# A fused state-space and long-convolution kernel: the first load in halves, table preparation shared out anew, K's spectrum ahead of V's

## The chip, the cores and the metric

One core of one Trainium2 chip. The metric is the device time of one execution in microseconds; the median of three runs of the kernel before is 444.19 (442.5 to 445.19). Times inside the kernel are counted from the start of the profiled span.

## The reference

Two branches read the same x and are mixed by a gate (2048 rows, 1024 channels, everything in bf16 outside, one batch):

```python
g = sigmoid((x * gate_w).sum(-1, keepdims=True))
# A: complex diagonal state space, P = 1024 states
Lam_bar = exp(dt * Lam);  B_bar = ((Lam_bar - 1) / Lam)[:, None] * Bmat
h_t = Lam_bar * h_(t-1) + x_t @ B_bar.T
a = 2 * real(h @ Cmat.T) + x * Dskip
# B: gated long convolution
k_shift = 4-tap causal filter of k (weights shift_k);  kv = k_shift * v
y = irfft(rfft(kv, 2S) * rfft(ssm_k, 2S))[:S] + kv * ssm_D
b = x * y
out = g * a + (1 - g) * b
```

## The kernel before

The convolution of branch B goes first, in eight chunks of 128 channels (`NC = 8`). It is a transform over 512-row blocks made of matrix products with tables of cosines and sines: `CF`, `SF` (forward; `NCF`, `NSF` are negated parts) and `CI`, `SI` (inverse, in two halves `h2`). For a chunk c the steps are:

- `load` fetches `kT`, `vT` (k and v transposed) and `kn` (the kernel ssm_k) by transposing DMAs on SyncE's queue.
- `taps` (lines 430 to 437): sixteen matmuls of `kT` with `dg`, four diagonal 128 x 128 matrices that hold the filter weights of the chunk, and two ScalarE evictions into `ks`. `dgs` (252 to 259) makes `dg`, four instructions, on VectorE for chunks 0 and 1 and on ScalarE for the others. Chunk 0 uses `first_times_v`, which multiplies by v straight from PSUM.
- `times_v`: two VectorE products, `lo` and `ks`.
- `fold_K`, `fold_V`: even and odd parts. `fold_V` multiplies by `PM`, four plus or minus identities; ScalarE evicts into `eok` and `eov`.
- `fwd_K(c, hf)`, `fwd_V(c, hf)`: the spectra, in two halves of frequencies. PSUM tiles `psk`, `psv`; ScalarE evicts them, two each, into `Kh` and `Vh`.
- `products(c, hf)` (511 to 544): the block products on VectorE, temporaries `t` from the rings `w4` (three buffers) and `u4` (four buffers), result `G`. It is a generator: its first step makes the products of lag 0, the rest comes later.
- `inverse(c)`: `psz`, sixteen matmuls a step with `CI` and `SI`, evicted to `cv` and written to DRAM.

After the eight chunks comes branch A: `Bu` (x times B), a rotated scan on VectorE over 16 pieces, `Cy` (states times C), the gate and the mixing. Its parameters are made by `state_params` (312 to 371), a generator on [128, 8] tiles: step 1 copies the columns into `pcol`, step 2 makes `dtv` and `rv` (ScalarE Exp) and `av`, `bv`, `thn` (VectorE), step 3 makes angles on VectorE (`thU`, `th_rq`, `th_fr`, `thU_rq`, `thU_fr`) and their sines and cosines on ScalarE (`th_fa` to `thU_cos`), and the rest makes the coefficients on VectorE (`rc` to `mc2i`). Exp and Sin lie in different ACT tables, and a table load stands wherever one follows the other. `turn_table` makes the rotation tables of branch A between the chunks.

The order of the work is written out by hand: `put` (line 97) ties every instruction to the one issued before it on the same engine, so the order of the calls is the order on each engine, and `step` and `run` drive the generators. A buffer of a ring is given to a new tile when its last reader is done; the reader's engine is then waited for. All PSUM work of a chunk shares three slots (`ps2`).

Before the loop stands the prologue: the first loads, nine matmuls on zeros (`raise_clock`), `dg` of chunk 0, the forward tables from `rqf` (fractions of turns; `hf` becomes |rqf| on VectorE and CF is its cosine), the first chunk up to its spectra, and `inverse_angles`, which makes the angles of the inverse tables in the rings `u4` and `w4`; the angles are read much later, by `inverse_table` in chunk 0 of the loop:

```python
def sincos(rq, n, sin_out, cos_out, sin_scale):
    fa = u4([128, n], F32, "fa")
    act(fa, rq, func=ACT.Abs)
    act(sin_out, rq, func=ACT.Sin, scale=sin_scale)
    act(cos_out, fa, func=ACT.Sin, bias=pih, scale=-TWO_PI)
```

Of the kernel before, what the change touches and what calls it, by code (L numbers as in the profile page):

```python
# [9 lines left out]
ALU = mybir.AluOpType  # L10
ACT = mybir.ActivationFunctionType
BF16 = mybir.dt.bfloat16
F32 = mybir.dt.float32
# [7 lines left out]
def kernel(  # L21
# [26 lines left out]
    nc = tc.nc  # L48
    xf = A_x.flatten_outer_dims()
    kf = B_k.flatten_outer_dims()  # L50
    vf = B_v.flatten_outer_dims()
    of = out.flatten_outer_dims()
    S, D = xf.shape
# [3 lines left out]
    ND = D // 128  # L57
    NP = P // 128
    NT = S // 128
    TB = 512  # L60
    NTB = S // TB
    NG = NP // 2
    NC = D // 128
# [5 lines left out]
    consts = pool("consts", 1)  # L69
# [4 lines left out]
    xt_pool = pool("xt", 2)  # L74
# [5 lines left out]
    def w4(shape, dt, name):  # L80
        return wk.tile(shape, dt, name=name, tag="w4")

    def u4(shape, dt, name):
        return wu.tile(shape, dt, name=name, tag="u4")
# [10 lines left out]
    def put(eng, f, *a, **kw):  # L95
        with tc.issue_after(prev[eng]) if eng in prev else nullcontext():
            i = f(*a, **kw)  # L97
        prev[eng] = getattr(i, "ins", i)
# [7 lines left out]
    V = nc.vector  # L106
# [4 lines left out]
    def ts(o, a, s1, s2, op0, op1=None):  # L111
        if op1 is None:
            put("dve", V.tensor_scalar, out=o, in0=a, scalar1=s1, scalar2=None, op0=op0)
        else:
            put("dve", V.tensor_scalar, out=o, in0=a, scalar1=s1, scalar2=s2, op0=op0, op1=op1)
# [4 lines left out]
    def act(o, i, **kw):  # L120
        put("act", nc.scalar.activation, out=o, in_=i, **kw)

    def load_t(o, i):
        put("sp", nc.sync.dma_start_transpose, out=o, in_=i)
# [36 lines left out]
    def load(which, c):  # L161
        cc = slice(c * 128, (c + 1) * 128)
        if which == "kn":

            t = ld.tile([128, NT, 128], BF16, name="kn", tag="ld")
            load_t(t, B_ssm_k[cc, :])
        else:
            t = ld.tile([128, S], BF16, name=which, tag="ld")
            load_t(t, (kf if which == "kT" else vf)[:, cc])
        lds[which, c] = t  # L170

    load("kT", 0)
# [8 lines left out]
            load_t(BT[g][:, c], src[g * 256:(g + 1) * 256, :])  # L181

    def load_xT(tb, home=None):
        xT = (home or xt_pool).tile([128, ND, TB], BF16, name="xT")
        load_t(xT, xf[tb * TB:(tb + 1) * TB, :])
        xTs[tb] = xT

# [12 lines left out]
    def flat(ap):  # L200
        return ap.rearrange("p a b -> p (a b)")
# [25 lines left out]
    ident = consts.tile([128, 128], BF16, name="ident")  # L227
# [12 lines left out]
    for k, v in enumerate((1.0, -1.0)):  # L240
        nc.gpsimd.affine_select(out=refl[:, k], in_=refl[:, k], pattern=[[1, 128]], base=-127, channel_multiplier=1,
                                compare_op=ALU.not_equal, fill=v)
# [9 lines left out]
    def dgs(c, on_dve=False):  # L252
        dg = ks_pool.tile([128, KS, 128], BF16, name="dg", bufs=1)
        for k in range(KS):
            if on_dve:
                ts(dg[:, k], ident, pcol[:, 4 + k, c:c + 1], None, ALU.mult)
            else:
                act(dg[:, k], ident, func=ACT.Identity, scale=pcol[:, 4 + k, c:c + 1])
        return dg

    dg0 = dgs(0, True)
    colm = consts.tile([128, 2], F32, name="colm")
    ts(colm, colm_i, 1.0 / 4096.0, None, ALU.mult)
    fr_ = u4([128, 512], F32, "fr_")
    copy(fr_, flat(fr_i))
    hf = u4([128, 2, 512], F32, "h")
    for mt in range(2):
        ts(hf[:, mt], fr_, colm[:, mt:mt + 1], None, ALU.mult)
    rqf = reduced(flat(hf), 1024)
    put("dve", V.scalar_tensor_tensor, out=flat(hf), in0=rqf, scalar=-1.0, in1=rqf, op0=ALU.mult, op1=ALU.max)  # L270
    PM = consts.tile([128, 2, 2, 128], BF16, name="PM")
    for a in range(2):
        for b in range(2):
            ts(PM[:, a, b], ident, -1.0 if a and b else 1.0, None, ALU.mult)

    inv = {}

# [5 lines left out]
        ts(inv["at0"], flat(colf), 511.0 / 2048.0, None, ALU.mult)  # L283

    def inverse_angles(h2):
        hi = (w4 if h2 else u4)([128, 2, 512], F32, "h")
        for k in range(2):
            fi = 2 * h2 + k
            ts(hi[:, k], trow[0], inv["col"][:, fi:fi + 1], inv["at0"][:, fi:fi + 1], ALU.mult, ALU.add)
        rq = (u4 if h2 else w4)([128, 1024], F32, "rq")  # L290
        ts(rq, flat(hi), MAGIC, -MAGIC, ALU.add, ALU.add)
        tt(flat(hi), flat(hi), rq, ALU.subtract)
        return flat(hi)
# [136 lines left out]
    def taps(c, dg):  # L430
        kT = lds.pop(("kT", c))
        ks = ks_pool.tile([128, S], BF16, name="ks")
        for h in range(2):
            ps = ps2([128, 2, 512], "taps")
            tap_sums(ps, kT, dg, h)
            act(ks[:, h * 1024:(h + 1) * 1024], flat(ps), func=ACT.Copy)
        kss[c] = ks
# [16 lines left out]
    def times_v(c):  # L454
        ks, vT = kss[c], lds.pop(("vT", c))
        lo = ks_pool.tile([128, 4, 256], BF16, name="lo", bufs=1)
        tt(lo, rev(ks), rev(vT), ALU.mult)
        khi, vhi = (ap.rearrange("p (b t) -> p b t", t=512)[:, :, 256:512] for ap in (ks, vT))
        tt(khi, khi, vhi, ALU.mult)
        kss[c] = ks, lo  # L460
# [14 lines left out]
    def fwd_K(c, hf):  # L475
        eo = eos["k", c]

        Kp = kv_pool.tile([128, 2, 4, 2, 128], BF16, name="Kh", tag="kvh")
        for f2 in range(2):
            fi = 2 * hf + f2  # L480
            fsl = slice(fi * 128, (fi + 1) * 128)
            fs2 = slice(f2 * 128, f2 * 128 + 128)
            ps = ps2([128, 2, 4, 128], "psk")
            for cc in range(2):
                tab = CF if cc == 0 else SF
                for mt in range(2):
                    mm(ps[:, cc], tab[:, mt, fsl], eo[:, mt, cc], mt == 0, False)
                for mt in range(2):
                    if cc == 0:
                        tb2 = SF[:, mt, fsl] if fi < 2 else NSF[:, mt, fs2]  # L490
                    else:
                        tb2 = NCF[:, mt, fs2] if fi < 2 else CF[:, mt, fsl]
                    mm(ps[:, cc, 1:4], tb2, eo[:, mt, 1 - cc, 0:3], False, mt == 1)
            act(Kp[:, :, :, f2], ps, func=ACT.Copy)
        KH[c, hf] = Kp

    def fwd_V(c, hf):
        eo = eos["v", c]
        Vp = kv_pool.tile([128, 2, 4, 2, 128], BF16, name="Vh", tag="kvh")
        for f2 in range(2):  # L500
            fi = 2 * hf + f2
            fsl = slice(fi * 128, (fi + 1) * 128)
            ps = ps2([128, 2, 4, 128], "psv")
            for cc in range(2):
                tab = CF if cc == 0 else SF
                for mt in range(2):
                    mm(ps[:, cc], tab[:, mt, fsl], eo[:, mt, cc], mt == 0, mt == 1)
            act(Vp[:, :, :, f2], ps, func=ACT.Copy, scale=2.0 / 1024.0)
        VH[c, hf] = Vp
# [217 lines left out]
    def step(gen):  # L727
        next(gen, None)
# [4 lines left out]

    none = iter(())
    act(flat(SF), rqf, func=ACT.Sin, scale=TWO_PI)
    act(flat(CF), flat(hf), func=ACT.Sin, bias=pih, scale=-TWO_PI)
    sp = state_params()
    first = first_times_v(0, dg0)
    step(first)
    step(sp)  # L740
    run(first)
    step(sp)
    dg1 = dgs(1, True)
    load("kT", 1)
    load("kn", 1)
# [7 lines left out]
    copy(trow[0], iota_i32([128, TB], [[1, TB]], 0, 0, "row"))  # L753
    inverse_cols()
    rqi = [inverse_angles(0), inverse_angles(1)]
    fwd_V(0, 0)
    fwd_K(0, 0)
    taps(1, dg1)
    step(sp)
    fwd_K(0, 1)  # L760
    fwd_V(0, 1)
# [2 lines left out]
    for c in range(NC):  # L764
        n, nn = c + 1, c + 2
        if n == NC:
            break
        if nn < NC:
            load("kT", nn)
            load("kn", nn)  # L770
        if c < NG:
            load_BT(c)
        elif c < NG + 2:
            load_xT(c - NG)
        if c == 0:
            tabs = []
        else:
            tabs = [turn_table(c - 1, u4)]
        if nn < NC:
            dg = dgs(nn)  # L780
        back = inverse(c - 1) if c else none
        p0, p1 = products(c, 0), products(c, 1)

        fold_K(n)
        for t in tabs:
            step(t)
        step(back)
        step(p0)
        times_v(n)
        for t in old:  # L790
            run(t)
        run(p0)
        fwd_K(n, 0)
        if c == 0:
            run(sp)
        for t in tabs:
            step(t)
        if nn < NC:
            load("vT", nn)
        fold_V(n)  # L800
        if c == 0:
            inverse_table(0, rqi[0])
        step(p1)
        run(back)
        for t in tabs:
            step(t)
        fwd_V(n, 0)
        if c == 0:
            inverse_table(1, rqi[1])
        for t in tabs:  # L810
            step(t)
        if nn < NC:
            taps(nn, dg)
        run(p1)
        fwd_K(n, 1)
        fwd_V(n, 1)
        for t in tabs:
            step(t)
        old = tabs
# [9 lines left out]
    c = NC - 1  # L829
# [4 lines left out]
    t = turn_table(NP - 2, w4)  # L834
# [128 lines left out]
```

## Time and profile before

| what | value |
|---|---|
| median of the runs shown | 444.19 us |
| the profiled execution: its time, its span | 444.19 us, 442.4 us |
| mean granted TensorE clock | 0.994 |
| TensorE busy | 423.1 us (96%) |
| VectorE busy | 421.9 us (95%) |
| ScalarE busy | 260.3 us (59%) |
| POOL busy | 27.1 us (6%) |
| first product of chunk 0 on VectorE | at 21.72 us |
| end of the chunk loop's work on TensorE, about | 197 us |

Busy times add the spans of instructions, so a busy matmul row is not an array at its peak. Everything that goes through a helper has line 97, so rows are told apart by the names of their tiles. A bracket behind a row of the timeline names the idle time ahead of it and what ended it.

### The profile page before, as it was taken

To read this page: it belongs to the slowest core of one execution; us is meant where nothing else is said; L and a number is where in the kernel's file an instruction comes from. 1 tells how busy PE (TensorE), PEld (TensorE's weight loads), DVE (VectorE), ACT (ScalarE), POOL (GpSimd) and SP (SyncE) were. 2 spreads that over 40 slices of the span, in tenths; PEclk is the share of its full clock that TensorE was granted. 3 is DMA by queue.
4 is the path that set the end of the run, shared out by engine and by line. 5 is a ranking of instruction groups with operands and counts; after the bars stand their busy time and mean duration, and the time that the engine had idled before them with its cause. 6 is when DMAs were issued, how large, how long until landed. Compare 5 with 4: busy or idle time off the path is not lost.

```text
span 442.4 us, 5684 instructions
## 1 busy us (share of the span) xinstructions
PE 423.1 (96%) x2104; PEld 199.4 (45%) x2142; DVE 421.9 (95%) x662; ACT 260.3 (59%) x320; POOL 27.1 (6%) x41
## 2 busy tenths in 40 slices
PE   8888899999999999979999999999999999999994
PEld 3434354544545454534444544444444444444442
DVE  7897999999999999999999999999999999999973
ACT  3796978979797979695552423443324432567102
POOL 2000000000000000000000000011011100223100
PEclk9998999999999999999999999999999999999999
DMA  7685294756558291135608941144474546297512
GB/s 144 144 134 105 49 184 100 140 111 149 125 102 184 60 205 24 25 68 100 115 12 159 176 135 24 25 119 111 99 172 96 147 139 166 38 207 162 118 45 98
DMA packets 128062, 49.94 MB, mean 113 GB/s; under 512 B 118169, under 2 KB 118177, under 8 KB 128034
## 3 DMA queue, kind: packets, MB, share of 16 engines
q1 hardware_dynamic: 123920, 42.22, 43.3%
q0 software_dynamic: 4032, 7.34, 9.6%
q8 instruction: 16, 0.26, 0.2%
q14 instruction: 12, 0.10, 0.1%
q10 hardware_dynamic: 82, 0.02, 0.0%
HBM read 8.67 MB, written 8.39 MB: 39 GB/s over the span
## 4 chain that ended last, share of the span: by engine, by line
PE 75%; DVE 12%; ACT 8%; issue 4%; DVEq 0%
PE bu L97 25%; PE psy L97 22%; PE psz L97 9%; PE psk L97 8%; DVE G L97 5%; DVE t L97 4%; PE taps L97 2%; PE foldk L97 2%; PE psv L97 2%; ACT Vh L97 2%; PE p L97 2%; PE foldv L97 2%; ACT eok L97 1%; ACT eov L97 1%; ACT Kh L97 1%
## 5 line engine op out<-in xcount | busy, mean ns | idle before, releaser
L97 PE MATMUL bu<-xT,BT 128*128 128x512 bf16 x499 | 111.6, 379 | 0.6
L97 DVE TENSOR_TENSOR t<-Kh,Vh 128x2048 bf16<-128x2048 bf16 (+3 forms) x128 | 102.3, 820 | 4.1 <-ACT SI L97 2.7
L97 PE MATMUL psy<-CT,hb 128*128 128x512 bf16 x470 | 105.2, 379 | 0.6
L97 PEld LDWEIGHTS <-BT 128*128 128x128 bf16 x512 | 50.0, 98 | 60.2
L97 PEld LDWEIGHTS <-hb 128*128 128x128 bf16 x512 | 49.9, 98 | 59.9
L97 DVE TENSOR_TENSOR G<-G,t 128x1536 bf16<-128x1536 bf16 (+2 forms) x144 | 69.4, 510 | 0.5
L97 ACT ACTIVATE U<-bu 128x1024 bf16<-128x1024 f32 x32 | 32.6, 1022 | 47.1 <-PE bu L97 42.3
L97 DVE TENSOR_TENSOR_SCAN W<-rv,init,A 128x512 bf16<-128x512 f32 x48 | 57.8, 1266 | 0.0
L97 PE MATMUL psz<-G,CI 128*128 128x512 bf16 x128 | 48.6, 379 | 2.0 <-DVE G L97 2.0
L97 PE MATMUL psz<-G,SI 128*128 128x512 bf16 x128 | 48.5, 379 | 0.0
L97 ACT ACTIVATE Kh<-psk 128x1024 bf16<-128x1024 f32 x32 | 32.6, 1028 | 10.7 <-PE psk L97 10.0
L97 ACT ACTIVATE ga<-psy,gcols 128x1024 bf16<-128x1024 f32 x8 | 8.9, 1114 | 46.3 <-PE psy L97 46.3
L97 PE MATMUL taps<-kT,dg 128*128 128x512 bf16 (+3 forms) x128 | 30.8, 385 | 1.6 <-ACT Vh L97 1.5
L97 ACT ACTIVATE Vh<-psv 128x1024 bf16<-128x1024 f32 x32 | 30.9, 1024 | 0.9 <-PE psv L97 0.9
L97 POOL DMA_DIRECT2D pbb<-gd x12 | 10.5, 871 | 342.4 <-ACT gd L97 330.3
L97 PE MATMUL psk<-eok,CF 128*128 128x512 bf16 (+1 forms) x96 | 26.5, 366 | 3.9 <-ACT eok L97 2.1
L97 ACT ACTIVATE cv<-psz 128x1024 bf16<-128x1024 f32 x16 | 16.4, 1027 | 23.0 <-PE psz L97 23.0
L97 PEld LDWEIGHTS <-CF 128*128 128x128 bf16 x160 | 15.7, 98 | 22.2 <-issue 7.0
L97 PE MATMUL psk<-eok,SF 128*128 128x512 bf16 (+1 forms) x89 | 24.7, 373 | 0.4
L97 ACT ACTIVATE BT<-psy,gcols 128x1024 bf16<-128x1024 f32 x6 | 6.7, 1111 | 30.6 <-PE psy L97 30.6
L97 PEld LDWEIGHTS <-SF 128*128 128x128 bf16 x160 | 15.9, 99 | 18.2 <-issue 3.5
L97 PE MATMUL psv<-eov,CF 128*128 128x512 bf16 x64 | 19.3, 379 | 3.0 <-ACT eov L97 2.2
(139 smaller groups left out, 570.0 us busy)
## 6 DMA issues: line engine op xcount, KB each, us to landing
cv_scr<-cv SPq DMA_DIRECT2D x32, 128.0 KB, 2.1
pbb<-cv_scr SPq DMA_DIRECT2D x12, 256.0 KB, 2.7
xr<-in_A_x_dram SPq DMA_DIRECT2D x12, 256.0 KB, 4.2
pbb<-gd POOLq DMA_DIRECT2D x12, 256.0 KB, 3.3
ga<-xr POOLq DMA_DIRECT2D x8, 256.0 KB, 3.3
out_dram<-ga SPq DMA_DIRECT2D x8, 256.0 KB, 2.0
out_dram<-BT SPq DMA_DIRECT2D x8, 256.0 KB, 2.0
BT<-cv_scr SPq DMA_DIRECT2D x4, 256.0 KB, 3.3
```

What stands on the lines that cost most here:

```text
L97: i = f(*a, **kw)
```

## The change

Five edits.

1. The first load of `kT` (chunk 0) becomes two transposing DMAs of half the rows each.
2. `PM` is made on POOL, by a memset and four selects, instead of four VectorE instructions; |rqf| is made on ScalarE (Abs) between SF and CF instead of on VectorE.
3. In the prologue `fwd_K(0, 0)` goes ahead of `fwd_V(0, 0)`. The first step of chunk 0's first `products` and `times_v(1)` move out of the loop to behind `taps(1)`, which leaves their places on VectorE as they were; step 2 of `state_params` moves behind them, next to step 3, and with it the ACT table load for Exp.
4. The angles of the inverse tables sit in a buffer of the pool of x (`xt_pool`), which is free until x is loaded in chunk 4; their temporary `rq` always comes from `w4`.
5. In the loop, `dgs(nn)` on ScalarE moves from ahead of `fold_K(n)` to behind `fwd_K(n, 0)`.

```diff
@@ load
-            load_t(t, (kf if which == "kT" else vf)[:, cc])
+            src = kf if which == "kT" else vf
+            if c == 0 and which == "kT":
+                load_t(t[:, 0:S // 2], src[0:S // 2, cc])
+                load_t(t[:, S // 2:], src[S // 2:, cc])
+            else:
+                load_t(t, src[:, cc])
@@ load_xT
-        xT = (home or xt_pool).tile([128, ND, TB], BF16, name="xT")
+        xT = (home or xt_pool).tile([128, ND, TB], BF16, name="xT", tag="xT")
@@ prologue
+    PM = consts.tile([128, 2, 2, 128], BF16, name="PM")
+    nc.gpsimd.memset(PM, 0.0)
+    for a in range(2):
+        for b in range(2):
+            nc.gpsimd.affine_select(out=PM[:, a, b], in_=PM[:, a, b], pattern=[[-1, 128]], base=0,
+                                    channel_multiplier=1, compare_op=ALU.not_equal, fill=-1.0 if a and b else 1.0)
...
     rqf = reduced(flat(hf), 1024)
-    put("dve", V.scalar_tensor_tensor, out=flat(hf), in0=rqf, scalar=-1.0, in1=rqf, op0=ALU.mult, op1=ALU.max)
-    PM = consts.tile([128, 2, 2, 128], BF16, name="PM")
-    for a in range(2):
-        for b in range(2):
-            ts(PM[:, a, b], ident, -1.0 if a and b else 1.0, None, ALU.mult)
@@ inverse_angles
-        hi = (w4 if h2 else u4)([128, 2, 512], F32, "h")
+        if h2 == 0:
+            inv["room"] = xt_pool.tile([128, 2, 2, 512], F32, name="h", tag="xT")
+        hi = inv["room"][:, h2]
...
-        rq = (u4 if h2 else w4)([128, 1024], F32, "rq")
+        rq = w4([128, 1024], F32, "rq")
@@ order of the prologue
     act(flat(SF), rqf, func=ACT.Sin, scale=TWO_PI)
+    act(flat(hf), rqf, func=ACT.Abs)
     act(flat(CF), flat(hf), func=ACT.Sin, bias=pih, scale=-TWO_PI)
...
     run(first)
-    step(sp)
     dg1 = dgs(1, True)
...
     rqi = [inverse_angles(0), inverse_angles(1)]
+    fwd_K(0, 0)
     fwd_V(0, 0)
-    fwd_K(0, 0)
     taps(1, dg1)
+    p0 = products(0, 0)
+    step(p0)
+    times_v(1)
+    step(sp)
     step(sp)
     fwd_K(0, 1)
     fwd_V(0, 1)
@@ the loop over chunks
-        if nn < NC:
-            dg = dgs(nn)
         back = inverse(c - 1) if c else none
-        p0, p1 = products(c, 0), products(c, 1)
+        if c:
+            p0 = products(c, 0)
+        p1 = products(c, 1)
         fold_K(n)
...
-        step(p0)
-        times_v(n)
+        if c:
+            step(p0)
+            times_v(n)
...
         run(p0)
         fwd_K(n, 0)
+        if nn < NC:
+            dg = dgs(nn)
```

## The prediction

> **What bounds the kernel now.** I read the page first, then the idle time of VectorE and TensorE with what ended it, then the timeline of the first 55 us engine by engine, and last the clock. All instructions of interest come from one helper (L97), so I go by tiles. Times are microseconds from the start of the span.
>
> ```profile
> span 442.4 us, 5684 instructions
> ...
> PE 423.1 (96%) x2104; PEld 199.4 (45%) x2142; DVE 421.9 (95%) x662; ACT 260.3 (59%) x320; POOL 27.1 (6%) x41
> ```
>
> Two engines are nearly full, so neither alone is the bound. The waits show where each of them has room:
>
> ```profile
> DVE t L97 <- ACT SI L97: 2.7, 1, 2.7
> ...
> DVE t L97 <- ACT Kh L97: 1.2, 1, 1.2
> ...
> PE psz L97 <- DVE G L97: 2.0, 1, 2.0
> ```
>
> VectorE waits 1.2 us for chunk 0's spectra, 2.7 us for SI, and then not again until 207 us. TensorE has one late wait, for G at 199.48:
>
> ```profile
> 199.48 0.38 PE L97 MATMUL psz<-G,CI 128*128 128x512 bf16 x1 [1.99 <-DVE G L97]
> ```
>
> After it TensorE has no gap until 428, and the chain of waits that ends last stays on it. So work that VectorE finishes x earlier before 199.48 brings the end forward by x, but by no more than those 1.99 us less whatever TensorE itself becomes late. Both leads are made, or lost, before about 51 us:
>
> ```profile
> 10.14 1.28 ACT L97 ACT_TABLE_LOAD   x1
> 20.67 1.02 ACT L97 ACTIVATE Kh<-psk 128x1024 bf16<-128x1024 f32 x1 [0.49 <-PE psk L97]
> 21.72 3.23 DVE L97 TENSOR_TENSOR t<-Kh,Vh 128x2048 bf16<-128x2048 bf16 x3 [1.16 <-ACT Kh L97]
> 25.26 1.28 ACT L97 ACT_TABLE_LOAD   x1
> 27.30 1.92 ACT L97 ACTIVATE Kh<-psk 128x1024 bf16<-128x1024 f32 x2
> 28.35 0.59 PE L97 MATMUL psv<-eov,CF 128*128 128x512 bf16 x2 [0.37 <-ACT Kh L97]
> 34.07 0.38 PE L97 MATMUL psk<-eok,CF 128*128 128x512 bf16 x1 [0.54 <-ACT eok L97]
> 38.77 1.02 ACT L97 ACTIVATE Kh<-psk 128x1024 bf16<-128x1024 f32 x1 [1.19 <-PE psk L97]
> 43.54 0.96 DVE L97 TENSOR_TENSOR t<-Kh,Vh 128x1536 bf16<-128x1536 bf16 x1 [2.65 <-ACT SI L97]
> 46.82 0.68 DVE L97 TENSOR_TENSOR t<-Kh,Vh 128x1024 bf16<-128x1024 bf16 x1
> 50.26 0.59 PE L97 MATMUL psk<-eok,CF 128*128 128x512 bf16 x2 [1.35 <-ACT ks L97]
> ```
>
> Read downwards: the first ACT table load stands in a free stretch of ScalarE, the second in a full one. From 38.77 to 50 ScalarE never idles, and TensorE's wait at 50.26 is for it.
>
> **The change, stretch by stretch.** *0 to 20 us.* Six raised matmuls start at 2.81 and take 0.43 each, so TensorE is free at 5.37; the taps start at 5.65, when the whole kT lands. A half lands sooner, but the gain is only up to 0.28 (0 if the half is no quicker); I take 0.22 and let foldk start at 9.80 for 10.02 (kn's bytes are all moved by 9.0). On VectorE the |x| step (1.22) and the four PM (0.49) go. That is hidden: its inverse angles end near 18.9 and must wait for Vh anyway; without that cover they would be worth 1.7. On ScalarE |x| costs one pass (nearest row: fa, 0.95 to the next start), CF ends at 10.9, and the table load (1.28), dtv and rv are gone from here, so eok starts at 11.0 for 12.13. eok's second half still waits for foldk (12.15), then eov at 13.15 and 14.07. PM on POOL costs a memset of about 0.5 and four selects of 0.27, done by 4.5 and needed at 12. The added DMA issue on SP's queue delays vT and kn by less than one issue (1.34). With K ahead of V, psk needs only eok: it starts when foldv ends, 13.8, and the 0.79 and 0.54 idle before psv in the old order go. psk 3.03, psv 1.73 (rows of the chain) end at 18.55; Kh at 15.5 and 17.03, Vh at 17.95 and 18.87 to 19.9. VectorE's first t starts at 19.93 instead of 21.72: 1.79 earlier.
>
> *20 to 30 us: the state step now stands on the path.* t, G, lo and ks take 5.56 as before and end at 25.48; the taps' ks on ScalarE ends at 23.2, the moved load and dtv at 24.75, so VectorE does not wait. But its eight small operations (av to thU_fr) now follow here. Before, three ran in the first 12 us and five behind the 1.16 wait; here, with a dependent pair 0.20 apart, they take 1.09. The next t starts at 26.57 for 27.28: the lead falls to 0.71. ScalarE waits in turn: rv for av (25.67), th_fa for th_fr (26.41), then the second load at 26.63. Kh followed that load by 2.04 (25.26 to 27.30), so it starts at 28.67, 1.37 later. Behind it in ScalarE's queue stand all spectra of half 1, and TensorE's second psv needs the room that Kh frees: 29.71 for 28.35. TensorE has nothing else from 25.9 on: 3.8 us idle.
>
> *30 to 51 us: the clock and dg.* Vh ends at 32.35. The four dg (1.15) no longer stand ahead of eok, so eok starts at 32.45 (32.08). What follows depends on the granted clock (the seventh number):
>
> ```profile
> 33.00:34.00 1.00, 0.38 (x1) 0.10 (x1) 0.97 (x5) 1.00 (x2) 0.00 (x0) 1.00 1.38 281
> 34.00:35.00 1.00, 0.93 (x4) 0.49 (x4) 0.90 (x9) 0.02 (x1) 0.00 (x0) 0.69 1.15 181
> ...
> 36.00:37.00 1.00, 1.00 (x4) 0.45 (x3) 0.93 (x4) 0.45 (x1) 0.00 (x0) 0.50 1.07 142
> ...
> 38.00:39.00 1.00, 1.00 (x8) 0.68 (x7) 1.00 (x2) 0.23 (x1) 0.00 (x0) 1.00 0.45 98
> ```
>
> After 2.1 us idle within 2.6 (31.55 to 34.07) the clock is halved from 34.3 to 37.7, and psk takes 4.3 instead of 3.03. With 3.8 us idle I expect the halving earlier, over foldk: its ten matmuls take about 3.7 instead of 2.2, foldk ends at 34.3, eok's second half at 35.4 (34.02), and psk then runs at full clock to 38.3. Its last Kh starts at 38.45 (38.77). Bounds: no halving, 37.3; halving over foldk and psk both, 39.75. The Trainium skill ("TensorE: Matmul & The Clock Gate", Part 1) says that activity is judged in fixed windows of about 3.4 us, so that an idle stretch longer than one always meets a halving; the 3.4 us at half clock here agree, and by it only the place is open.
>
> The dg, now after this Kh, add 1.15 ahead of eov: CI of the first inverse table ends at 45.4 (44.55), and the ks that TensorE awaits at 50.26 lets it go at 51.1: TensorE is 0.85 late. VectorE starts half 1's products at 35.75 (36.46). The wait for SI goes, since the angles no longer sit in the ring of t. But the fa that the table makes still does: the t at 46.82 takes its room and needs CI done. VectorE gets there at 43.4 and waits 2.1 to 45.45. It still is 1.37 ahead of before.
>
> *51 us to the end.* In the loop dg moves from ahead of eok to ahead of eov. ScalarE idles 2.35 after eov in each chunk, waiting for psz (the cv at 67.63), which covers the 1.15; without the cover it would cost up to 1.15 in each of five chunks. VectorE's tightest input is Vh of chunk 2, ready at 72.14 and used at 74.56: margin 2.42, against 1.37 + 0.85 = 2.22, so the lead just fits. At 199.48 VectorE is 1.37 early, and TensorE's 1.99 of room has shrunk by 0.85 to 1.14. The smaller counts: **1.1 us**. The profiled execution took 444.19, also the median, 1.79 beyond its span; span 441.3, time **443.0**.
>
> **The rivals.** *No halving.* Kh at 37.3 makes TensorE 0.3 early, with room for 2.3, and CI0 ends at 44.3, VectorE 2.5 early: 444.19 - 2.3 = 441.9. For it: 1.5 us idle between 14.2 and 15.9 caused none. Against: 3.8 is far more.
>
> *The gain is eaten.* Halving over psk as well (Kh at 39.75), or kn landing 1.3 late behind three queued loads, leaves both leads near 0: 444.2. For it: this very psk was halved before. Against: foldk ahead of it is dense work.
>
> *Slower: the two table loads in the full queue.* They now stand one behind the other between ks and Kh, where everything of half 1 waits. If each held ScalarE for twice its 1.28, Kh would start at 31.2 and the later one at 41.0; TensorE would be 3.4 late against 1.99 of room: 444.19 + 1.4 = 445.6. It decides once the later Kh passes 39.8. Against: 25.26 + 1.28 = 26.54, and th_sin runs at 26.56. The Trainium skill ("ScalarE: Activation LUTs", "What ACT_TABLE_LOAD costs") adds a drain of about 1.38 to each 1.28; by that, an estimate of 2.8 more for two loads, the time would be 445.8. The trace has 0.02 there, so I keep this unlikely.
>
> **How the numbers follow.** Forecast 0.5, no halving 0.18, eaten 0.15, slower 0.1; 0.07 is left for what I have not seen. Executions of the kernel before spread from 442.5 to 445.19, so I take 1.7 off the fastest case and, since the slowest is itself unlikely, add only 0.4 to that: 440.2 to 446.0. A 1% change (4.4 us), about what a measurement of this kernel can tell from none, would need all of TensorE's room twice over, or a late Kh past 43: faster 0.05, within 1% 0.89, slower 0.06.
>
> **What would show it.** Right: first t near 19.9; VectorE's next t after thU_fr near 26.6; Kh of half 1 near 28.7 behind two loads; a TensorE gap of 3 to 4 us before the psv at 29.7, and half clock just after; VectorE waiting about 2 us for CI instead of SI; a wait before the late psz of about 0.2 instead of 1.99. Wrong: a first t after 20.6, a late Kh after 39.8, or TensorE gaps between 60 and 190 at eov or psv.

## The result, and the profile after

The changed kernel is slower: 445.81 us median against 444.18 us for the kernel before, a ratio of 1.0052 (95% interval 1.0035 to 1.0069). The forecast was 443.0, faster than before, with a range of 440.2 to 446.0: the time lies inside the range, and the direction is wrong. The profiled execution of the changed kernel took 446.97, at a span of 445.2 and a mean clock of 0.989. Two later profiles, both of the state step moved alone, are of slow executions (902.23 and 457.61 us), which are in no ratio; of these only order and gaps are read.

The page of the changed kernel:

```profile
span 445.2 us, 5731 instructions
...
PE 424.9 (95%) x2142; PEld 199.0 (45%) x2142; DVE 421.1 (95%) x657; ACT 262.3 (59%) x321; POOL 28.5 (6%) x46
```

The profiled execution is 2.8 us longer than that of the kernel before. VectorE is busy 0.8 us less, so on it all of that is idle time. TensorE is busy 1.8 us more; this can't be divided between idle time and slower matmuls, since the page of before lacks 38 of its 2142 matmul records. The waits of VectorE, then of TensorE, in the changed kernel (engine, line, what was waited for, total, times, longest):

```profile
DVE t L97 <- ACT CI L97: 3.2, 1, 3.2
...
DVE t L97 <- ACT Vh L97: 1.6, 1, 1.6
DVE t L97 <- ACT TC L97: 1.5, 2, 1.3
...
DVE TCi L97 <- ACT TCi L97: 0.3, 1, 0.3
```

```profile
PE psv L97 <- ACT Kh L97: 4.2, 2, 3.7
PE psv L97 <- ACT eov L97: 2.0, 2, 1.4
PE psz L97 <- DVE G L97: 1.9, 1, 1.9
...
PE foldk L97 <- DMA kn<-in_B_ssm_k_dram: 1.0, 1, 1.0
```

The wait for SI is gone, and one for CI stands in its place, as forecast. New are the wait for kn, the 1.3 us for TC and the 1.4 us for eov (0.28 before); and the wait for G is still 1.9, where 0.2 was forecast. The timeline of the changed kernel, the rows that answer to those of before:

```profile
20.35 3.23 DVE L97 TENSOR_TENSOR t<-Kh,Vh 128x2048 bf16<-128x2048 bf16 x3 [1.61 <-ACT Vh L97]
23.69 1.28 ACT L97 ACT_TABLE_LOAD   x1
26.10 0.21 ACT L97 ACTIVATE rv<-av 128x8 f32<-128x8 f32 x1 [0.91 <-DVE av L97]
26.86 0.21 ACT L97 ACTIVATE th_fa<-th_fr 128x8 f32<-128x8 f32 x1 [0.56 <-DVE th_fr L97]
27.03 0.95 DVE L97 TENSOR_TENSOR t<-Kh,Vh 128x1536 bf16<-128x1536 bf16 x1
27.09 1.28 ACT L97 ACT_TABLE_LOAD   x1
28.39 0.21 ACT L97 ACTIVATE th_sin<-th_fr 128x8 f32<-128x8 f32 x1
29.12 1.92 ACT L97 ACTIVATE Kh<-psk 128x1024 bf16<-128x1024 f32 x2
30.18 1.01 PE L97 MATMUL psv<-eov,CF 128*128 128x512 bf16 x2 [3.68 <-ACT Kh L97]
40.12 1.02 ACT L97 ACTIVATE Kh<-psk 128x1024 bf16<-128x1024 f32 x1 [0.49 <-PE psk L97]
41.03 1.26 ACT L97 ACTIVATE dg<-ident,pcol 128x128 bf16<-128x128 bf16 x4
42.20 1.92 ACT L97 ACTIVATE eov<-foldv 128x1024 bf16<-128x1024 f32 x2
47.08 0.69 DVE L97 TENSOR_TENSOR t<-Kh,Vh 128x1024 bf16<-128x1024 bf16 x1 [3.17 <-ACT CI L97]
52.76 0.59 PE L97 MATMUL psk<-eok,CF 128*128 128x512 bf16 x2 [1.35 <-ACT ks L97]
72.83 0.69 DVE L97 TENSOR_TENSOR t<-Kh,Vh 128x1024 bf16<-128x1024 bf16 x1 [1.34 <-ACT TC L97]
201.86 0.38 PE L97 MATMUL psz<-G,CI 128*128 128x512 bf16 x1 [1.88 <-DVE G L97]
```

The first t is 1.37 earlier than before, and by 27.03 that lead has shrunk to 0.25, because the eight small state operations now stand on VectorE's path. Kh of half 1 starts 1.82 later (29.12 for 27.30). From the end of the taps' ks, at 23.67, to this Kh ScalarE takes 5.45 us, where before it took 2.16. Of the 3.29 more, 1.28 are the added table load and 1.47 are waits for av and th_fr, which stand behind VectorE's products. TensorE idles 3.68 us, and from here on everything is late: the last Kh by 1.35, TensorE at ks by 2.50, the late psz by 2.38. In the stretches of one microsecond (the seventh number is the granted clock) the half clock covers all of foldk:

```profile
29.00:30.00 1.00, 0.00 (x0) 0.00 (x0) 1.00 (x3) 1.00 (x2) 0.00 (x0) 0.63 1.31 276
30.00:31.00 1.00, 0.82 (x3) 0.26 (x3) 1.00 (x3) 1.00 (x3) 0.00 (x0) 0.50 1.23 278
...
35.00:36.00 1.00, 1.00 (x4) 0.17 (x3) 0.83 (x7) 0.00 (x0) 0.00 (x0) 0.50 0.00 0
36.00:37.00 1.00, 0.38 (x1) 0.05 (x2) 0.97 (x3) 0.97 (x1) 0.00 (x0) 0.96 0.00 0
```

That is 6.8 us (29.3 to 36.0), twice the 3.4 of before. It is not the same in every execution. Of thirteen, two had a mean clock of 0.994 to 0.995 and took 444.46 and 444.89; four at 0.989 took 446.6 to 447.9; seven between took 445.5 to 446.6. The profiled one is among the long ones.

### The profile page after: what moved, and what is told of

It is laid out like the page before. It is cut to its first block, busy times and chain, and to the rows that moved or that the text cites. A ratio compares the mean times of both kernels' runs of the same rounds, so it can differ in the third digit from the quotient of the medians.

```text
span 445.2 us, 5731 instructions
## 1 busy us (share of the span) xinstructions
PE 424.9 (95%) x2142; PEld 199.0 (45%) x2142; DVE 421.1 (95%) x657; ACT 262.3 (59%) x321; POOL 28.5 (6%) x46
## 3 DMA queue, kind: packets, MB, share of 16 engines
q1 hardware_dynamic: 123952, 42.22, 41.8%
## 4 chain that ended last, share of the span: by engine, by line
PE 61%; DVE 28%; ACT 5%; issue 2%; SPq 1%; DMA 1%; DVEq 0%
PE bu L97 25%; PE psy L97 23%; DVE G L97 12%; DVE t L97 12%; PE psz L97 5%; PE psk L97 3%; PE p L97 2%; PE foldk L97 2%; DVE hr L97 1%; SPq L97 1%; ACT Vh L97 1%; DMA kn<-in_B_ssm_k_dram 1%; ACT Kh L97 1%; PE foldv L97 1%; PE psv L97 1%
```

## The experiments

The theories that the expectations name: A, the state step's two table loads make Kh, and by it ScalarE's chain, late, partly by way of the clock, with dg on top (the rows above add the waits for av and th_fr to the loads; no run tries the two apart); B, the half loads and the late kn are the loss; C, VectorE's wait for CI is; D, dg's new place alone is. A began as "TensorE is late, and VectorE is held by the ring of t at TC"; hr_elsewhere refuted that last part. What took its place, that all hangs on the start of eov, was tested by the second run of the state step alone, by dg_alone and by dg_twice, which were written down after it.

All runs, with what their profiles show. "Kh" is the start of the Kh of half 1 of chunk 0, "eov" the start of chunk 1's eov on ScalarE, "psz" the late psz that waits for G; "half clock" is what falls between 24 us and that eov.

| kernel | ratio (95% interval) | half clock | Kh | eov | psz | psz - eov | profiled time - eov |
|---|---|---|---|---|---|---|---|
| before | 1 | 3.4 us, psk | 27.30 | 39.69 | 199.48 | 159.79 | 404.50 |
| changed | 1.0052 (1.0035-1.0069) | 6.8 us, foldk | 29.12 | 42.20 | 201.86 | 159.66 | 404.77 |
| dg0_back | 1.0045 (1.0023-1.0068) | 3.4 us | 29.30 | 40.25 | 199.94 | 159.69 | 404.72 |
| state_back | 0.9974 (0.9960-0.9987) | none | 26.62 | 37.34 | 197.02 | 159.68 | 404.76 |
| gap_filled | 1.0033 (1.0020-1.0046) | none | 28.91 | 39.62 | 199.30 | 159.68 | 404.66 |
| fa_elsewhere | 1.0076 (1.0049-1.0102) | 3.4 us | 29.04 | 40.99 | 200.66 | 159.67 | 404.69 |
| whole_load | 1.0033 (1.0018-1.0048) | 3.4 us | 28.14 | 40.09 | 199.75 | 159.66 | 404.69 |
| room_alone | 0.9989 (0.9972-1.0006) | none | 27.29 | 38.00 | 197.68 | 159.68 | 404.64 |
| exp_first | 0.9951 (0.9931-0.9972) | none | 25.28 | 36.84 | 196.49 | 159.65 | 404.73 |
| exp_first_dg0 | 0.9976 (0.9958-0.9993) | 3.4 us | 25.36 | 38.37 | 198.05 | 159.68 | 404.82 |
| hr_elsewhere | 1.0064 (1.0041-1.0087) | none | 29.04 | 39.76 | 199.40 | 159.64 | 404.93 |
| exp_first_whole | 0.9949 (0.9928-0.9969) | none | 25.78 | 37.34 | 197.01 | 159.67 | 404.73 |
| exp_first_whole_hr | 0.9949 (0.9930-0.9968) | none | 23.75 | 35.31 | 194.96 | 159.65 | 404.79 |
| dg_alone | 0.9996 (0.9981-1.0011) | none | 27.29 | 38.01 | 197.77 | 159.76 | 404.81 |
| dg_twice | 1.0081 (1.0049-1.0113) | 3.4 us | 28.97 | 42.16 | 201.79 | 159.63 | 404.74 |

Two columns carry the explanation. psz comes 159.63 to 159.79 us after eov in fifteen profiles whose eov differ by 6.9 us: in these kernels, when that one eviction starts on ScalarE, the rest is fixed. Half clock behind eov does not change it: seven of the fifteen have another 3.4 us of it there, before 49 us. And without half clock before eov, eov follows Kh by 10.71 to 10.72 us in room_alone, state_back, gap_filled, hr_elsewhere and dg_alone, so at full clock a late Kh is passed on whole. (With Exp first it is 11.56 in three profiles; there Kh is so early that it waits for psk in between.) Of the two runs of the state step alone only order and gaps are read, so they are not in the table.

**The state step put back.** In the changed kernel:

```diff
     run(first)
+    step(sp)
     dg1 = dgs(1, True)
...
     taps(1, dg1)
+    step(sp)
     p0 = products(0, 0)
     step(p0)
     times_v(1)
-    step(sp)
-    step(sp)
```

> The changed kernel, with both state steps (Exp load, dtv to thn; angles and their sines) back where they stood in the kernel before; all other edits stay. Theory A: only one table load stands between ks and the Kh of half 1, which starts near 27.0 for 29.12; the first t is up to 1 us later than 20.35, because load, dtv and rv now delay eok; TensorE's gap ahead of psv falls from 3.68 to about 2; foldk runs mostly at full clock, the last Kh of chunk 1's half 0 starts between 37.0 and 38.8 for 40.12; with dg still ahead of eov TensorE is 0 to 1 us late near 51 and the end is 1.5 to 2.5 us earlier than in the changed kernel: ratio 0.999 to 1.002. Theory B (loads): the ratio stays at 1.005. Theory D (dg alone): 1.0045 or more, since dg keeps its new place.

Measured: 442.08 us, ratio 0.9974, faster than the kernel before. The order on ScalarE in this kernel:

```profile
24.59 1.28 ACT L97 ACT_TABLE_LOAD   x1
...
26.62 1.92 ACT L97 ACTIVATE Kh<-psk 128x1024 bf16<-128x1024 f32 x2
...
35.25 1.02 ACT L97 ACTIVATE Kh<-psk 128x1024 bf16<-128x1024 f32 x1 [0.49 <-PE psk L97]
36.17 1.26 ACT L97 ACTIVATE dg<-ident,pcol 128x128 bf16<-128x128 bf16 x4
37.34 1.92 ACT L97 ACTIVATE eov<-foldv 128x1024 bf16<-128x1024 f32 x2
```

One load is left ahead of Kh, TensorE's gap there is 0.37 instead of 3.68 us, and eov starts 4.86 earlier than in the profile of the changed kernel. The time fell by more than expected. The other edits together bring 0.3%; the state step's place turns that into a loss.

**The state step alone.** The kernel before, with the opposite move: the step goes to its new place (products(0, 0) and times_v(1) taken ahead with it, as in the change). It was run twice.

> The kernel before, with one edit of the change alone: step 2 of the state parameters (Exp load, dtv, av, bv, rv, thn) moved, with step 3, behind the first products and products with v of chunk 1. Theory A: eok, eov and with them the first t come 0.5 to 0.9 us earlier (the Exp load no longer stands ahead of eok), then both table loads stand between ks and Kh: Kh of half 1 at 29.0 to 29.8 for 27.30, TensorE idle over 3 us before the second psv, half clock over foldk, the last Kh of chunk 1 at 39 to 41 for 38.77, VectorE 0.7 to 2 us late; time 0.8 to 2.2 us over the kernel before: ratio 1.002 to 1.005. If the loss came from the other edits: ratio 0.998 to 1.001.

> The kernel before with the state step moved alone, once more for its profile. Theory A (the loss is the start of eov on ScalarE, late by the two table loads): Kh of half 1 at 29 to 29.8, TensorE idle over 3 us before the second psv, half clock over foldk in most executions, eov of chunk 1 at 41 to 42.5 for 39.69, G of the late psz 159.7 after that, time 445.3 to 447. If eov starts below 40.5 and the time is still above 445, the loss goes another way.

Measured: ratios 1.0069 (1.0047 to 1.0091) and 1.0065 (1.0037 to 1.0094), so this edit alone costs about as much as the whole change, and more than the expected 1.002 to 1.005. In the second profile (clock 0.95 where it is not halved) Kh starts at 29.92, TensorE idles 3.27 us ahead of the second psv, half clock follows from 30.6 to 34, and eov starts at 40.97: the expected way.

**The gap filled.** In the changed kernel, ahead of the second psv of half 1, work for TensorE that nobody reads:

```diff
             ps = ps2([128, 2, 4, 128], "psv")
+            if (c, hf, f2) == (0, 1, 1):
+                keep = ps1("p2")
+                for _ in range(15):
+                    mm(keep, ident, CF[:, 0], True, True)
```

> The changed kernel, with 15 matmuls of 128x512 on a table, into a PSUM bank that nobody reads, in TensorE's 3.68 us gap ahead of the second psv of half 1 (3.2 us of work at full clock). Nothing else moves. Theory A says that most of the loss of the state step comes through the clock: without the idle stretch foldk runs at full clock (0.22 a matmul for 0.43) and ends near 33.3 instead of 35.9, eok's second half starts near 34.0 for 36.03, the last Kh near 38.2 for 40.12, and the end is about 1.9 us earlier than in the changed kernel: ratio 1.000 to 1.002. If the clock is not the carrier (the lateness comes straight from the table loads, by way of Kh and Vh on ScalarE), the Kh at 40.12 moves by less than 0.5 and the ratio stays at 1.004 to 1.005.

Measured: 444.70, ratio 1.0033; between the two expectations. The profile agrees with the first one on the clock:

```profile
29.00:30.00 1.00, 0.56 (x4) 0.16 (x3) 1.00 (x3) 1.00 (x2) 0.00 (x0) 1.00 1.35 253
30.00:31.00 1.00, 1.00 (x5) 0.45 (x5) 1.00 (x3) 1.00 (x2) 0.00 (x0) 1.00 1.09 143
```

The clock is not halved, and the last Kh comes at 37.54. But the median is only 1.1 us below that of the changed kernel, and the intervals of the two ratios overlap. The changed kernel's gap costs a long halving in some executions and, to judge by the mean clocks of 0.994 to 0.995 above, little or none in others. What is left, 0.33%, is the direct way: Kh is 1.62 later than in room_alone (28.91 for 27.29), whose ScalarE order is that of the kernel before, and at full clock eov is 1.62 later too (39.62 for 38.00).

**dg of chunk 0 put back.** In the changed kernel `dg = dgs(nn)` stands ahead of `fold_K(n)` for `c == 0`, and behind `fwd_K(n, 0)` for the others.

> The changed kernel, with the four dg of chunk 0 alone put back ahead of fold_K. Theory A (a late chain on ScalarE: the late K spectrum of half 1 plus dg ahead of eov make TensorE 2.50 us late at its wait for ks near 52.8): ScalarE idles 0.68 and 1.23 around eok, so dg costs nothing there; the Kh at 40.12 stays, eov starts at 41.05 for 42.20, the first CI ends at 45.9, TensorE's wait for ks ends near 51.6 (1.35 late against the kernel before instead of 2.50), and the end comes 1.1 to 1.5 us earlier than in the changed kernel: ratio to the kernel before 1.002 to 1.003. Theory B (the half loads and the late kn are the loss) and theory C (VectorE's 3.17 us wait for CI through the ring is the loss by itself) differ: B, nothing but the dg's place moves and the ratio stays at 1.005; C, VectorE gains the same 1.15 and the ratio goes to 1.0025 as in A, but TensorE's lateness near 51.6 would be without effect.

Measured: 444.97, ratio 1.0045; 0.84 us less in the median than the changed kernel, somewhat under the expected 1.1 to 1.5, and the intervals overlap. eov follows Kh after 10.95 us, against 11.95 in fa_elsewhere, where dg stands behind Kh and the clock is halved as long, though 1 us earlier: ahead of eok, dg falls into the time in which ScalarE waits for the slow foldk.

**dg alone**, moved in the kernel before, and **dg twice**, written a second time in the changed kernel's chunk 0:

```diff
+        if c == 0:
+            for k in range(KS):
+                act(dg[:, k], ident, func=ACT.Identity, scale=pcol[:, 4 + k, nn:nn + 1])
         if c == 0:
             run(sp)
```

> The kernel before, with the dg edit alone: dg on ScalarE behind the first K spectrum instead of ahead of fold_K, in all chunks. Theory A, by the start of eov: without dg ahead of it eok starts at about 30.9 for 32.08, TensorE's gap ahead of psk shrinks from 2.1 us to about 1 and the clock is not halved there; the last Kh starts near 36 for 38.77, dg adds 1.15, eov starts at 38.0 to 38.4, 1.3 to 1.7 earlier than in the profile before (39.69, half clock) and level with an execution at full clock (38.0). So the time is 442.5 to 443.0 in nearly all executions: ratio 0.997 to 0.9995. If dg's 1.15 us ahead of eov were simply added, as the prediction had it: 1.0025.

> The changed kernel, with the four dg of chunk 0's turn written a second time, ahead of eov: 1.15 us more on ScalarE there and nothing else. Theory A, by the start of eov: CI, ks, TC, TCi and with them VectorE and TensorE all come 1.15 later, since both are held to ScalarE's chain; 446.7 to 447.2 for 445.81, ratio 1.007 to 1.0085. If VectorE and TensorE had room of their own there (1.9 us ahead of the late psz): no more than 0.4 us, ratio 1.005 to 1.006.

Measured: dg_alone 443.33, ratio 0.9996, 0.3 us above the expected times, with an interval that excludes 1.0025; eov at 38.01. At full clock the four dg cost the same on either side of Kh, 38.01 here and 38.00 in room_alone. dg_twice: 446.95, ratio 1.0081. Its profile has one halving ahead of eov, as that of fa_elsewhere, and against that one eov is 1.17 later (42.16 for 40.99) and psz 1.13 (201.79 for 200.66): pushing eov pushes the end, one for one (the profiled executions took 446.90 and 445.68).

**Two rings relieved.** fa_elsewhere puts the |angles| of the inverse tables, and hr_elsewhere the angles of the first four turn tables, into the second buffer of x:

```diff
-        fa = u4([128, n], F32, "fa")
...
+        if h2 == 0:
+            inv["fa"] = xt_pool.tile([128, 2, 1024], F32, name="fa2", tag="xT")
...
```

```diff
-        hr = home([128, 2, TB], F32, "hr")
+        if pi < 4:
+            if "hr" not in inv:
+                inv["hr"] = xt_pool.tile([128, 2, 2, TB], F32, name="hr2", tag="xT")
+            hr = inv["hr"][:, pi % 2]
...
```

> The changed kernel, with the |angles| (fa) of the inverse tables in the second buffer of the pool of x, free until chunk 4, instead of the ring of t. VectorE's longest wait, 3.17 us for CI at 47.08, goes. Theory A: nothing is gained at the end. VectorE arrives some 3.1 us earlier at the t of 72.83, which takes the room of the turn table's angles, and waits there for TC about 4.4 instead of 1.34, since TC follows cv on TensorE's late chain: the time stays within 0.5 us of the changed kernel, ratio 1.004 to 1.006. Theory C (this wait is the loss): VectorE keeps its 3 us, the wait for G near 201.9 shrinks from 1.88 to nothing, and the time falls by about 1.9 us, ratio 1.001.

> The changed kernel, with the angles (hr) of the first four turn tables in the second buffer of the pool of x instead of the ring of t, so that no t of chunk 1 has to wait until TC is made. Theory A, with the ring at TC as the place where VectorE's lead is lost: the 1.34 us wait of the t at 72.83 goes, VectorE keeps what it had at 47 (0.3 late to 1.0 early, depending on how long the clock is halved), TensorE stays 1.3 to 2.5 us late near 52 and uses up its room of 1.99 us: the wait for G near 201.9 shrinks from 1.88 to under 1, and the time falls by 1.0 to 2.2 us against the changed kernel: ratio 1.000 to 1.003. If VectorE is held at another place too, or the ring is not the limit, the wait for G stays at 1.9 and the ratio at 1.005.

Measured: 445.83, ratio 1.0076, and 445.86, ratio 1.0064: neither gains. The wait for CI, the longest of VectorE in the chunks, is worth nothing, as theory A said. With fa out of the ring VectorE waits longer at TC, 2.51 us (4.4 were expected; the halving was shorter in this profile):

```profile
71.62 0.69 DVE L97 TENSOR_TENSOR t<-Kh,Vh 128x1024 bf16<-128x1024 bf16 x1 [2.51 <-ACT TC L97]
```

The second expectation missed. With hr out of the ring the wait for TC goes, and VectorE waits at the next tie instead, 1.56 us where the changed kernel had 0.33:

```profile
79.78 0.43 DVE L97 TENSOR_TENSOR TCi<-TCi,m 128x512 bf16<-128x512 bf16 x1 [1.56 <-ACT TCi L97]
```

Here VectorE needs the tables themselves, no buffer: TCi is scaled on ScalarE behind work that TensorE feeds. The rings of t were not the limit here; VectorE is tied to ScalarE's chain at the tables, whatever it gained before.

**The angles' room alone**, edit 4 in the kernel before:

> The kernel before, with one edit of the change alone: the angles of the inverse tables in the buffer of x, their rq always from w4. Theory A, with the ring as the limit: VectorE's wait of 2.65 us for SI goes and it is up to 2.3 us early near 47 (a short wait for CI, about 0.4, takes its place), but ScalarE's and TensorE's chain is where it was, so at the t of 71.15 the ring of t is held by the turn table until TC is made (70.3 in the kernel before): of the lead 0.84 us stay. G of the late psz comes 0.84 earlier, ratio 0.998. If nothing limits on the way, VectorE keeps 2.3 us and TensorE's room of 1.99 us is filled: ratio 0.9955. If the SI wait was worth nothing: 1.000.

Measured: 443.53, ratio 0.9989; its interval holds both the expected 0.998 and no change. The wait for SI goes, and the waits for TC and TCi take VectorE's lead: at full clock the late psz comes at 197.68 here and at 197.77 in dg_alone, which still waits for SI.

**The whole first load**, in the changed kernel:

> The changed kernel, with the first load of kT whole again, one transposing DMA instead of two. Theory A: vT and kn are issued 0.5 to 1.2 us earlier, foldk of chunk 0 starts at 9.8 for 10.2, the first t near 19.95, and everything up to the stretch of the table loads comes 0.2 to 0.45 us earlier; the table loads still stand between ks and Kh. The time falls by 0.2 to 0.5 us against the changed kernel: ratio 1.003 to 1.005. Theory B (the half loads are the loss): the ratio falls to 1.000 or below.

Measured: 445.20, ratio 1.0033: as theory A had it, 0.6 us below the changed kernel in the median where it said 0.2 to 0.5; the intervals overlap. The SyncE queue of the changed kernel, and then of this one:

```profile
0.74 2.59 SPq L97 DMA_TRANSPOSE kT<-in_B_k_dram  x2
3.38 2.42 SPq L97 DMA_TRANSPOSE vT<-in_B_v_dram  x1
5.84 2.29 SPq L97 DMA_TRANSPOSE kn<-in_B_ssm_k_dram  x1
```

```profile
0.74 1.34 SPq L97 DMA_TRANSPOSE kT<-in_B_k_dram  x1
2.13 2.58 SPq L97 DMA_TRANSPOSE vT<-in_B_v_dram  x1
4.76 2.12 SPq L97 DMA_TRANSPOSE kn<-in_B_ssm_k_dram  x1
```

The two halves hold the queue about twice as long as the one whole load, so vT goes 1.25 and kn 1.08 later. The taps start at 5.35 with the halves and 5.30 without: nothing was won by them. foldk starts at 10.23 with, 9.05 without.

**Exp ahead of everything.** The changed kernel, with the first two state steps in the first 8 us, before SF needs its Sin table, and the angles ahead of the second taps:

```diff
-    raise_clock(6)
+    raise_clock(4)
...
-    rqf = reduced(flat(hf), 1024)
+    sp = state_params()
+    step(sp)
+    raise_clock(2)
+    rqf = u4([128, 1024], F32, "rq")
+    ts(rqf, flat(hf), MAGIC, -MAGIC, ALU.add, ALU.add)
+    step(sp)
+    tt(rqf, flat(hf), rqf, ALU.subtract)
...
+    step(sp)
     taps(1, dg1)
...
-    step(sp)
-    step(sp)
```

> The changed kernel, with the first two state steps (the four columns, dtv, av, bv, rv, thn) in the first 8 us, where ScalarE has nothing but its first table load: Exp is loaded first and Sin behind it, ahead of SF, so that no table load stands between the chunks at all; the step with the angles stands ahead of the second taps, where VectorE waits for Vh. All other edits as in the changed kernel, dg behind Kh too. Theory A: SF starts up to 0.6 us later than at 8.02, the first t stays between 20.2 and 20.8, the next t comes at 25.8 to 26.4 for 27.03, Kh of half 1 at 24 to 25 for 29.12, TensorE has no gap over 1 us before the second psv, no halving of the clock there, and VectorE runs on without a wait for SI, CI or TC. It is then some 1 us earlier at the late psz than the kernel with the state steps put back (197.02), whose VectorE waits 1.74 us for dtv near 12: time 440.6 to 441.6, ratio 0.992 to 0.9945. If the loss were not the place of the loads but dg or the half loads, the time would stay within 1 us of the changed kernel.

> As the kernel with Exp first, and the four dg of chunk 0 back ahead of fold_K. Theory A: with the table loads gone VectorE sets the end, not ScalarE's chain, so dg's place is worth nothing any more: TensorE's wait for ks near 47 ends 0.5 to 1.2 us earlier, but the time stays within 0.4 us of the kernel without this edit. If ScalarE's chain still sets the end, the time falls by 0.5 us or more, as it did in the changed kernel (445.81 to 444.97).

Measured: 441.67, ratio 0.9951, and with dg0 ahead 442.70, ratio 0.9976. exp_first beats both kernels, by less than expected: its first t came at 21.47, because TensorE idled 0.81 us for the columns' DMA and took 5.07 us for its sixteen taps, where the changed kernel has 1.90 for each 8. That pace is like half clock in part, but the granted clock is recorded as 1.00 there, so the cause of it is not shown. The expectation for dg0 was wrong, at 1 us instead of under 0.4: dg ahead of fold_K delays eok, TensorE idles 1.13 and 0.54 us, and in that profile the clock is halved from 33.6 to 37.0, over psk.

The next two keep all six raised matmuls ahead of the columns and load kT whole; the second also has hr out of the ring.

> The kernel with Exp first, mended in two places: all six raised matmuls stand ahead of the columns' matmul, so that TensorE does not idle 0.81 us there and run the taps at a low clock, and the first load of kT is whole again. Theory A: taps at 5.6, first t at 19.4 to 20.4 for 21.47, next t near 25.2 to 26, Kh of half 1 near 24; no wait of VectorE after that. VectorE is 1 to 2 us earlier at the late psz than the 196.49 of the kernel with Exp first; time 439.5 to 441.0 for 441.67: ratio 0.990 to 0.993. If something else bounds by then (a load of chunk 1, ScalarE's chain): 0.994 to 0.995.

> The same kernel, with the angles of the first four turn tables out of the ring of t as well. Theory A: if ScalarE's and TensorE's chain keeps up with VectorE there is no wait for TC to remove, and the time stays within 0.4 us of the kernel without this edit; where VectorE does wait for TC in it, that wait goes and the time falls by up to its length, at most 1 us.

Measured: 440.70, ratio 0.9949, and 440.58, ratio 0.9949, 0.5% faster than the kernel before; no certain gain over exp_first, and none from hr, as expected of hr. The gain over exp_first was missed in the profile of the first: the columns' matmul waited 1.05 us for its DMA and the sixteen taps took 5.31 us, so the first t is at 21.97. In the second it waited 0.50, the taps took 3.83, and the first t is at 19.94, with eov at 35.31, the earliest of all. Between that t and the late psz VectorE shows no wait in either.

## Why the prediction was wrong

**The start.** Forecast for the first t 19.93, measured 20.35. The halves were priced at a gain of 0.22 and a delay to kn that costs nothing. Against the whole load they gained nothing (taps at 5.35 for 5.30), and foldk started 0.43 later than forecast (1.18 later than with the whole load). K ahead of V, and ScalarE freed of the load, went as forecast.

**The state step.** Sizes were right: eight operations 1.12 (1.09), the next t 27.03 (26.57), Kh 29.12 (28.67), the gap 3.68 (3.8). What lies between is the 0.42 of the start. The two loads took 1.28 each, and th_sin ran 0.02 after the second. The Trainium skill ("ScalarE: Activation LUTs", "What ACT_TABLE_LOAD costs") adds a drain of some 1.38 to a switch; no such time stands in the row here. So the rival whose time came nearest, 445.6 by loads of twice their price, had the place right and the mechanism wrong; that its time is 0.2 from the measured one is luck.

**The half clock.** It came over foldk, as forecast, but 6.8 us long in the profile, and the last Kh at 40.12 for 38.45. With a shorter one the size was nearly right: 38.90 in fa_elsewhere, in whose order nothing ahead of it differs. I had written that a gap of this length always meets a halving, from the window of 3.4 us that the Trainium skill gives ("TensorE: Matmul & The Clock Gate", Part 1). The length agrees: 3.4 us, or twice that. But hr_elsewhere has the same 3.68 us gap and no half clock until 41.8. That fits the same page of the Trainium skill, by which the windows run freely: a gap a little longer than one need not cover one. So the "always" that I worked out from the page was wrong by the runs. The one case that spoke for no halving, put at 1.5 us of idle time, is 1.33 us by its rows (0.79 and 0.54).

**The step that failed is the last one**, where leads were carried past 51 us. It gave VectorE a lead of 1.37 of its own and TensorE a lateness of 0.85 to be paid from 1.99 us of room, and took Vh of chunk 2, with 2.42 of margin, for VectorE's tightest input. Two ties are tighter. In the kernel before:

```profile
69.59 0.71 ACT L97 ACTIVATE TC<-hr,pih 128x512 bf16<-128x512 f32 x1
71.15 0.69 DVE L97 TENSOR_TENSOR t<-Kh,Vh 128x1024 bf16<-128x1024 bf16 x1
...
79.56 0.73 ACT L97 ACTIVATE TSi<-TS,c2r 128x512 bf16<-128x512 bf16 x1
80.44 0.42 DVE L97 TENSOR_TENSOR TSi<-TSi,m 128x512 bf16<-128x512 bf16 x1
```

And in the changed kernel:

```profile
82.06 0.73 ACT L97 ACTIVATE TSi<-TS,c2r 128x512 bf16<-128x512 bf16 x1
82.82 0.42 DVE L97 TENSOR_TENSOR TSi<-TSi,m 128x512 bf16<-128x512 bf16 x1 [0.18 <-ACT TSi L97]
```

The t at 71.15 takes the room of the turn table's angles, and TC was ready at 70.30: margin 0.85, against the 2.22 that were asked of it. Behind it VectorE takes the tables TCi and TSi themselves. Its TSi row starts 0.76 or 0.77 us after that of ScalarE in thirteen of the fifteen profiles, and 0.87 and 0.88 in the other two, dg_alone and the kernel before: there the margin was 0.1. From this row the late psz is 119.01 to 119.06 us away in all fifteen. So no lead that VectorE has ahead of 80 us is worth more than 0.1 us while ScalarE's TSi stays where it is, and a later TSi moves the late psz with it. Both inputs follow from ScalarE's chain, which runs from eov to ks without idling (42.20 to 53.49 in the changed kernel), and through TensorE's unbroken chain behind ks (52.76 to 73.6); ScalarE's TSi stands 39.86 us behind eov there, and 39.87 before. So VectorE cannot lead where that chain is late, and the room ahead of the late psz was none. It stayed at 1.88 (1.99 before) because both sides of it moved together; G was 2.38 late where it was forecast 1.37 early. dg_twice shows it by pushing, state_back by pulling, fa_elsewhere and hr_elsewhere by taking away a wait and gaining nothing. By this reading, the forecast's own numbers give eov at 38.45 + 0.92 + 1.15 = 40.5, and a time of 40.5 + 404.7 = 445.2: slower, as measured.

**What was left as rivals.** "No halving" would not have been 441.9: gap_filled has none, with its late Kh at 37.54, and takes 444.70. A late Kh after 39.8, which I had named as the sign of being wrong, came in the profile of the changed kernel, but gap_filled shows that the kernel is slower without it too. "The gain is eaten" was right that no lead would be left, but not about the way: no halving came over psk, and the late kn cost foldk 0.43. That dg in the later chunks costs nothing was right: the wait ahead of cv fell from 2.35 to 1.20, and dg_alone has a ratio of 0.9996.

## What to carry to other kernels

Follow a lead or a lateness through the next tie between the engines before adding it up: two engines that each show slack late in the kernel may both be waiting on a third one's chain, and then the slack is no room. Look for the one row whose distance to the end is the same in every variant; here it was an eviction on an engine that is only 59% busy. And a table switch, with the small operations that hang on it, belongs where its engine is idle: with this step in the first 8 us, and its angles ahead of the second taps, a loss of 0.5% became a gain of 0.5%.

## What the hardware showed that I had not expected

- A gap of 3.68 us on TensorE came with half clock for 6.8 us, 3.4 us, or not at all before 41.8 us (profiles of the changed kernel, fa_elsewhere, hr_elsewhere). Gaps of 1.44 and 0.54 within 2 us also led to 3.4 us of half clock (state_back, 39.7 to 43.1).
- A transposing DMA of half the rows, first in the SyncE queue, held it about as long as one of all rows: 2.59 us for two halves, 1.34 for the whole (profiles of the changed kernel and of whole_load).
- The four dg of the prologue on VectorE took 1.04 us while POOL made its selects for PM, and 0.74 in the kernel before; that the selects are the cause was not tried apart.
